# Seven block products for eight in the first FFN product of token chunks 2 and 3

## Chip, cores and metric

The kernel runs on one core of a Trainium2 chip. The metric is device time in microseconds. Where "clock" is given it is the granted TensorE clock, 1.0 being full speed.

## The reference, cut to what matters

```python
# x: 1 x 2048 x 640; wqkv: 640 x 1920; wo: 640 x 640; w1: 640 x 1728; w2: 1728 x 640, all bf16
xn = _layernorm(x)
q, k, v = split_heads(xn @ wqkv)                    # 32 heads of 20
phi = lambda t: where(t > 0, t + 1, exp(t)) + 1e-6
pq, pk = phi(q), phi(k)
kv  = einsum("bhsd,bhse->bhde", pk, v)
z   = einsum("bhsd->bhd", pk)                       # sum of the keys over all tokens
num = einsum("bhqd,bhde->bhqe", pq, kv)
den = einsum("bhqd,bhd->bhq", pq, z)[..., None] + 1e-6
s = merge_heads(num / den) @ wo
h = maximum(xn @ w1, 0)                             # the first FFN product
g = silu(h @ w2)
return x + s * g
```

The 2048 tokens are 16 tiles of 128, or four chunks (0 to 3) of 512. The kernel computes `h` transposed, in blocks of 128 of w1's columns by one chunk: five matmuls of 512 columns each, since 640 = 5 x 128.

## The kernel before

A small scheduler gives each operation the waits that its reads and writes need; each engine works through its own queue in the order of the program. These parts matter (cuts marked `# ...`).

```python
# z: the running sum of the key tiles, one GpSimd addition for each of the 16 tiles
def z_add():
    t = zpend.pop(0)
    sc.op("POOL", lambda eng: eng.tensor_tensor(out=zacc, in0=zacc, in1=pk[:, t, :], op=ALU.add), ...)

def K_fin(t):                      # phi of a key tile, two VectorE instructions with all inputs in SBUF
    sc.op("DVE", ... tensor_scalar(out=e_, in0=e_, scalar1=1.0, scalar2=1e-6, op0=ALU.min, op1=ALU.add) ...)
    sc.op("DVE", ... tensor_tensor(out=pk[:, t, :], in0=e_, in1=r_, op=ALU.add) ...)
    zpend.append(t)

def Q_block(j, f):                 # 5 matmuls, one exp on ScalarE, two VectorE instructions
    # ...                          # the second of them reads PSUM
    sc.op("DVE", ... scalar_tensor_tensor(out=pqT[:, f, schunk(j)], in0=ps[b], scalar=1.0 + 1e-6,
                                          in1=e_, op0=ALU.add, op1=ALU.max) ...)

def H_block(j, f):                 # 5 matmuls and one relu on ScalarE: a block of h
    # ...

# where things stand: chunk j's H blocks with Q blocks between them; key tiles, statistics and z by position
kat = [{5: 4, 7: 5, 9: 6, 11: 7}, {7: 8, 11: 9, 15: 10, 19: 11}, {6: 12, 9: 13, 12: 14, 15: 15}, {}]
lnat = [{}, {0: 8, 3: 9, 6: 10, 9: 11}, {0: 12, 2: 13, 4: 14, 6: 15}, {}]
zfrom = [9, 99, 10, 0]
for j in range(J):
    for n, item in enumerate(plans[j]):
        # ... Q_block or H_block, LN_stats, LN_norm, K_mm, K_exp, K_relu, K_fin
        if n >= zfrom[j] and zpend and j < J - 1:
            z_add()
        # ...
        if j == J - 1:
            while zpend:
                z_add()
            if n == 1:
                z_split()          # z as a sum of two bf16 numbers
            # ...
            if n == 9:
                z_col()            # ten one-column matmuls turn z into a column
```

The Gram product later in the kernel already uses a seven-product scheme (`seven`).

## Time and profile before

| | kernel before |
|---|---|
| time, median of runs | 210.3 us (209.55 to 210.85) |
| span of the profiled run | 208.9 us |
| TensorE busy | 205.2 us (98%), 1,377 matmuls |
| VectorE busy | 160.3 us (77%) |
| ScalarE busy | 109.7 us (53%) |
| GpSimd busy | 45.8 us (22%) |

TensorE is the bound. (PSUM, below, is the memory that matmuls write to; SBUF is the other on-chip memory.) This is GpSimd's timeline of the kernel before (start, duration, line, operation, out<-in, shapes, count):

```profile
73.28 18.19 POOL L528 TENSOR_TENSOR wv_sb<-wv_sb,reg 128x640 f32<-128x640 f32 x12
```

And this is VectorE's timeline of the same kernel, inside that time (a bracket at the end gives the idle time before the instruction and who ended it):

```profile
80.74 0.33 DVE L550 TENSOR_SCALAR regE<-regE 128x640 bf16<-128x640 bf16 x1 [1.29 <-ACT regE L534]
81.40 1.26 DVE L552 TENSOR_TENSOR reg<-regE 128x640 bf16<-128x640 bf16 x1 [0.34 <-ACT regE L534]
85.33 0.33 DVE L550 TENSOR_SCALAR regE<-regE 128x640 bf16<-128x640 bf16 x1 [2.67 <-ACT regE L534]
```

Twelve of the sixteen additions run in a block, and VectorE then has idle time in front of its instructions. Some are lengthened (1.26 us), some not (0.33 us), and nobody waits for them.

### The profile page before, as it was taken

The page shows a single profiled execution, that of the slowest core. Times are in us where ns is not written, and L with a number is a line of the kernel's source. Part 1 is how long each engine was busy: PE and PEld are TensorE (multiplying, and loading weights), DVE is VectorE, ACT ScalarE, POOL GpSimd, SP SyncE. Part 2 cuts the span into 40 slices and gives each one's busy share as a digit, 9 for nine tenths or more (in the row PEclk, how much of TensorE's full clock was granted, in tenths as well). Part 3 has the DMA queues.
Part 4 walks back from the last instruction along what each step waited for, and adds up shares of the span by engine and source line. Part 5 has one row for each costly group of instructions (what it writes and reads, how often), then busy time and mean ns, then how long its engine had stood idle before and what let it go on. Part 6 is the DMA issues. An engine that isn't in the chain of part 4 may idle for free.

```text
span 208.9 us, 3582 instructions
## 1 busy us (share of the span) xinstructions
PE 205.2 (98%) x1377; PEld 126.6 (61%) x1377; DVE 160.3 (77%) x321; ACT 109.7 (53%) x215; POOL 45.8 (22%) x71
## 2 busy tenths in 40 slices
PE   8999999999999999999999999999999999999995
PEld 7755554555454555444447777767777777777773
DVE  3988965798855995369597785897888989797465
ACT  5697767466565566655653424462435254353531
POOL 2278701111017399990000000000000000000001
PEclk9999999999999999999999999999999999999999
DMA  6987499221001334000189999346911010110103
GB/s 197 359 295 155 90 315 90 50 45 31 3 0 22 72 79 145 0 2 0 28 285 261 322 282 332 107 120 231 319 51 63 0 66 28 38 36 30 63 3 126
DMA packets 30359, 24.74 MB, mean 118 GB/s; under 512 B 12037, under 2 KB 30341, under 8 KB 30341
## 3 DMA queue, kind: packets, MB, share of 16 engines
q1 hardware_dynamic: 27013, 20.26, 34.8%
q10 hardware_dynamic: 3328, 4.24, 6.2%
q8 instruction: 11, 0.18, 0.4%
q14 instruction: 7, 0.06, 0.1%
HBM read 15.81 MB, written 5.24 MB: 101 GB/s over the span
## 4 chain that ended last, share of the span: by engine, by line
PE 97%; DMA 1%; DVE 1%; issue 0%
PE psT L798 40%; PE psT L591 27%; PE psT L517 11%; PE psT L570 10%; PE psT L1217 3%; PE psT L1301 2%; DMA reg<-in_A_x_dram 1%; PE psT L610 1%; PE psT L1008 1%; PE psT L491 1%; PE psT L982 1%; PE psT L703 1%; DVE stats L436 0%; DVE reg L1205 0%; DVE reg L1210 0%; DVE reg L484 0%
## 5 line engine op out<-in xcount | busy, mean ns | idle before, releaser
L591 PE MATMUL psT<-reg 128*128 128x512 bf16 x195 | 46.0, 379 | 0.0
L595 ACT ACTIVATE regH<-psT 128x512 bf16<-128x512 f32 x52 | 30.8, 602 | 17.2 <-PE psT L591 17.2
L798 PE MATMUL psT<-reg,regH 128*128 128x320 bf16 (+1 forms) x224 | 34.3, 299 | 0.0
L591 PEld LDWEIGHTS psT<-reg 128*128 128x128 bf16 x195 | 18.9, 98 | 21.8 <-issue 0.4
L798 PE MATMUL psT<-reg 128*128 128x320 bf16 (+1 forms) x164 | 27.2, 299 | 0.0
L798 PEld LDWEIGHTS psT<-reg,regH 128*128 128x128 bf16 (+1 forms) x224 | 21.9, 98 | 8.5
L1210 POOL TENSOR_TENSOR reg<-reg 128x224 bf16<-128x224 bf16 x1 | 0.6, 608 | 112.2 <-DVE reg L1205 112.2
L570 PE MATMUL psT<-reg 128*128 128x512 bf16 x100 | 24.8, 379 | 0.0
L1042 ACT ACTIVATE wv_sb<-psT 128x320 bf16<-128x320 f32 x28 | 11.3, 436 | 25.3 <-PE psT L798 15.5
L528 POOL TENSOR_TENSOR wv_sb<-wv_sb,reg 128x640 f32<-128x640 f32 x16 | 23.1, 1442 | 1.9 <-DVE reg L552 1.0
L743 DVE TENSOR_TENSOR psT<-psT,reg 128x320 f32<-128x320 f32 x30 | 14.3, 495 | 11.5 <-PE psT L798 11.2
L534 ACT ACTIVATE regE<-psT 128x640 bf16<-128x640 f32 x24 | 15.6, 701 | 9.1 <-PE psT L517 9.1
L798 PEld LDWEIGHTS psT<-reg 128*128 128x128 f16 (+1 forms) x164 | 16.0, 98 | 6.4
L805 ACT ACTIVATE psT<-psT 128x320 f32<-128x320 f32 x32 | 13.6, 426 | 10.8 <-PE psT L798 10.3
L517 PE MATMUL psT<-reg 128*128 128x320 bf16 x120 | 18.3, 299 | 0.0
L570 PEld LDWEIGHTS psT<-reg 128*128 128x128 bf16 x100 | 9.8, 98 | 11.6
L805 ACT ACTIVATE reg<-psT 128x320 f32<-128x320 f32 (+1 forms) x22 | 9.6, 435 | 13.1 <-PE psT L798 13.1
L576 ACT ACTIVATE regE<-psT 128x512 bf16<-128x512 f32 x20 | 12.0, 598 | 8.5 <-PE psT L570 8.5
L436 DVE BATCH_NORM_STATS2 stats<-reg 128x6 f32<-128x320 bf16 x32 | 14.1, 475 | 2.3 <-DMA reg<-in_A_x_dram 2.3
L517 PEld LDWEIGHTS psT<-reg 128*128 128x128 bf16 x120 | 11.7, 98 | 6.5
L577 DVE TENSOR_SCALAR regE<-regE 128x512 bf16<-128x512 bf16 x20 | 7.7, 386 | 9.6 <-ACT regE L576 9.5
L591 PE MATMUL psT<-regX,reg 128*128 128x512 bf16 x65 | 14.8, 379 | 0.0
(106 smaller groups left out, 300.0 us busy)
## 6 DMA issues: line engine op xcount, KB each, us to landing
scr<-rden SPq DMA_DIRECT2D x4, 640.0 KB, 9.4
reg<-in_A_x_dram SPq DMA_DIRECT2D x4, 640.0 KB, 6.3
out_dram<-reg SPq DMA_DIRECT2D x15, 160.0 KB, 1.9
reg<-in_A_x_dram SPq DMA_DIRECT2D x14, 160.0 KB, 3.4
reg<-scr SPq DMA_DIRECT2D x2, 640.0 KB, 7.5
regE<-scr SPq DMA_DIRECT2D x2, 640.0 KB, 8.0
reg<-in_B_w_dram ACTq DMA_DIRECT2D x1, 1040.0 KB, 6.6
reg<-in_A_wo_dram SPq DMA_DIRECT2D x6, 160.0 KB, 3.2
```

The source lines that it names most:

```text
L436: sc.op("DVE", lambda eng: eng.bn_stats(stats[:, t, a, :], xv[:, HN * a:HN * (a + 1)]), R=[("xin", t % XR)], W=[("stats", t, a)])
L517: fns.append(lambda eng, a=a, k=k, lhs=lhs: eng.matmul(ps[b + a][:, 0:HN], lhsT=lhs, rhs=wk[:, k, HN * a:HN * (a + 1)], start=(k == 0), st ...
L528: sc.op("POOL", lambda eng: eng.tensor_tensor(out=zacc, in0=zacc, in1=pk[:, t, :], op=ALU.add), R=[("zacc",), ("pk", t)], W=[("zacc",)])
L534: sc.op("ACT", lambda eng: eng.activation(out=o_.rearrange("p (a n) -> p a n", a=2), in_=ps2(b, HN), func=func, scale=scale), R=[("ps", b) ...
L570: sc.group("PE", [(lambda eng, k=k: eng.matmul(ps[b], lhsT=wq[:, k, P * f:P * (f + 1)], rhs=xnT[:, j, k, :], start=(k == 0), stop=(k == C ...
L576: sc.op("ACT", lambda eng: eng.activation(out=e_, in_=ps[b], func=ACTF.Exp), R=[("ps", b)], W=[("er_e", es)])
L591: a = sc.group("PE", [(lambda eng, k=k: eng.matmul(ps[b], lhsT=w1_col(k, P * f, P), rhs=src[:, k, :], start=(k == 0), stop=(k == C - 1))) ...
L595: sc.op("ACT", lambda eng: eng.activation(out=hT[:, f, schunk(j)], in_=ps[b], func=ACTF.Relu), R=[("ps", b)], W=[("hT", j, f)])
L743: sc.op("DVE", lambda eng: eng.tensor_tensor(out=out, in0=in0, in1=in1, op=op), R=R, W=W, extra=extra)
L798: sc.group("PE", [(lambda eng, k=k, lhs=lhs, rhs=rhs: eng.matmul(ps[b][:, 0:HN], lhsT=lhs, rhs=rhs, start=(start and k == 0), stop=(k == n ...
L805: sc.op("ACT", lambda eng: eng.activation(out=dst, in_=ps[b][:, 0:HN], func=ACTF.Copy), R=[("ps", b)], W=[dkey], extra=extra)
L1042: sc.op("ACT", lambda eng: eng.activation(out=g[:, HN * n:HN * (n + 1)], in_=ps[b][:, 0:HN], func=ACTF.Silu), R=[("ps", b)], W=[("g", sl, ...
```

## The change

The intent is to save TensorE work. Column blocks i and i + 6 of w1 (i = 0 to 5) with token chunks 2 and 3 form a two by two block product; over the first four of the five pieces of 128 it takes seven products of two matmuls for eight, and the fifth piece is added in the plain way: 18 matmuls for 20. Six such units replace 24 blocks. They need sums of blocks of w1 (`h_S`) and of x (`h_T`), so w1 is kept by pairs of column blocks (seven loads for three), and chunks 2 and 3 must be normalised, transposed and summed before the first unit. For that, the statistics and norms of tiles 8 and 9 move up into chunk 0's stage, and chunk 1's stage gets those of tiles 10 to 15 and the key tiles 8 to 15. Q's evacuation (the passes that bring a matmul's result out of PSUM) goes partly to ScalarE, and the z additions are issued after the stage. Buffers are rehoused, among them that of chunk 1's column scales and chunk 0's row scales.

```diff
-    FC = [0, 4 * P, 7 * P, FF]
-    w1_p = [reg5[:, C * FC[i]:C * FC[i + 1]]... for i in range(3)]
+    NW = 7
+    WL = [2 * P * d for d in range(NW)] + [FF]
+    w1_p = [reg5[:, C * WL[d]:C * WL[d + 1]]... for d in range(NW)]
 ...
-    w1_load(2, "ACT")
     K_relu(0, 2)
+    w1_load(3, NW, "SP", [("ACT", sc.count["ACT"] - 1)])
 ...
     # Q_block: the second pass of its evacuation moves from VectorE (PSUM) to ScalarE, VectorE adds in SBUF
+        def f_relu():
+            sc.op("ACT", ... activation(out=pqT[:, f, schunk(j)], in_=ps[b], func=ACTF.Relu) ...)
+        def f_sum():
+            sc.op("DVE", ... tensor_scalar(out=e_, in0=e_, ..., op0=ALU.min, op1=ALU.add) ...)
+            tt(pqT[:, f, schunk(j)], e_, pqT[:, f, schunk(j)], ALU.add, ...)
 ...
+    def h_S(d, i):       # sums of w1 blocks: A21 + A22, that - A11, A12 - that, A11 - A21
+    def h_T(i):          # sums of x:         B12 - B11, B22 - B12, that + B11, B21 - that
 ...
+    def h_unit(i):       # seven products; product 7 reuses the bank that the sum after product 6 reads
+        def s6():
+            mm(6, ba)
+            tt(ps[bc], ps[ba], s5, ALU.add, [("ps", ba), ("ps", bc), skey], [("ps", bc)])
+        # ...
+        def s7():
+            mm(7, ba)
+            cp(ps[bd], ("ps", bd), ba)
 ...
-    kat = [{5: 4, 7: 5, 9: 6, 11: 7}, {7: 8, 11: 9, 15: 10, 19: 11}, {6: 12, 9: 13, 12: 14, 15: 15}, {}]
-    lnat = [{}, {0: 8, 3: 9, 6: 10, 9: 11}, {0: 12, 2: 13, 4: 14, 6: 15}, {}]
-    zfrom = [9, 99, 10, 0]
-    for j in range(J):
+    kat = [{5: 4, 7: 5, 9: 6, 11: 7}, {2: 8, 5: 9, 8: 10, 11: 11, 14: 12, 16: 13, 18: 14, 20: 15}]
+    lnat = [{9: 8, 11: 9}, {0: 10, 2: 11, 5: 12, 8: 13, 11: 14, 13: 15}]
+    for j in range(2):
 ...
-            if n >= zfrom[j] and zpend and j < J - 1:
-                z_add()
 ...
+    Q_block(2, 0, 1)
+    Q_block(2, 1, 3)
+    while zpend:
+        z_add()
+    z_split()
 ...
+    for i, u in enumerate(units):        # s1 s5 [filler] s6 s2 [filler] s7 s3 s1-of-next s4
```

## The prediction

> **What bounds the kernel now.** I read the page first: busy shares, the slices, the chain that ended last.
>
> ```profile
> PE   8999999999999999999999999999999999999995
> DVE  3988965798855995369597785897888989797465
> POOL 2278701111017399990000000000000000000001
> PEclk9999999999999999999999999999999999999999
> ...
> PE 97%; DMA 1%; DVE 1%; issue 0%
> ```
>
> One digit is a fortieth of 208.9 us, 5.2 us. TensorE is full in every slice from the second on and its clock is never throttled; the chain is 97% TensorE. The chain in order of time has no gap above 0.02 us between 12 and 206 us, so today TensorE's stream of matmuls is the time. One piece of it gives the price of a matmul:
>
> ```profile
> 11.93 6.47 PE psT L591 x30
> ...
> 103.27 6.58 PE psT L591 x30
> ```
>
> 30 matmuls of 512 columns in 6.47 us are 0.216 us each. (The groups' 379 ns is latency; matmuls overlap.) In the same way ten of 320 columns take 1.36 us, 0.136 each. So every 512-column matmul that goes is worth 0.216 us, as long as nothing else begins to hold TensorE up. Next I asked which engine could. A table by stages gives VectorE's busy time:
>
> ```profile
> 32.50:58.60 26.10, 26.10 (x137) 13.29 (x136) 20.74 (x55) 16.01 (x27) 3.47 (x8) 1.00 0.20 40
> 58.60:87.80 29.20, 29.20 (x152) 14.70 (x150) 19.53 (x37) 18.50 (x31) 20.64 (x28) 1.00 0.23 57
> ```
>
> Columns after the length: TensorE, weight loads, VectorE, ScalarE, GpSimd (instructions in brackets). In the first stage VectorE is 79% busy and GpSimd idles; in the second VectorE has far fewer instructions (37 for 55) but nearly the same busy time, because GpSimd is working. The timelines of those two engines, 18 to 27 us, show why:
>
> ```profile
> 18.61 1.16 DVE L455 TENSOR_SCALAR reg<-reg,mv,rsy 128x640 bf16<-128x640 bf16 x1 [0.46 <-POOL rsy L444]
> 19.68 1.52 DVE L550 TENSOR_SCALAR regE<-regE 128x640 bf16<-128x640 bf16 x1
> 21.23 1.61 DVE L552 TENSOR_TENSOR reg<-regE 128x640 bf16<-128x640 bf16 x1
> 22.77 0.31 DVE L550 TENSOR_SCALAR regE<-regE 128x640 bf16<-128x640 bf16 x1
> 23.11 1.61 DVE L552 TENSOR_TENSOR reg<-regE 128x640 bf16<-128x640 bf16 x1
> ```
>
> ```profile
> 18.54 1.03 POOL L856 TENSOR_TENSOR wv_sb<-ident,rsy 128x512 f16<-128x512 bf16 x1
> 19.54 2.95 POOL L528 TENSOR_TENSOR wv_sb<-wv_sb,reg 128x640 f32<-128x640 f32 x2
> 22.98 1.40 POOL L528 TENSOR_TENSOR wv_sb<-wv_sb,reg 128x640 f32<-128x640 f32 x1 [0.49 <-DVE reg L552]
> 24.87 1.47 POOL L528 TENSOR_TENSOR wv_sb<-wv_sb,reg 128x640 f32<-128x640 f32 x1 [0.49 <-DVE reg L552]
> ```
>
> L550 takes 0.31 us when GpSimd waits and 1.52 when an L528 (the running sum of the keys, z) runs; L552 takes 0.49 undisturbed elsewhere and 1.61 here. Each L528 holds back one VectorE instruction until it ends, and the next L528 gets in before VectorE's next one. Five GpSimd passes here lengthen five VectorE instructions by 0.8, 1.2, 1.1, 1.1 and 1.1 us: **about 1.06 us a pass**. L579, which reads PSUM, keeps its 0.69 us while L528 runs (76.3 us).
>
> **What the Trainium skill says.** "SBUF — State Buffer", section "Who interferes with whom": VectorE and GpSimd share one port pair under an exclusive lock; a tensor_scalar in a two-port mode, or a tensor_tensor with both inputs in SBUF against a GpSimd operation that reads SBUF, waits for the whole other instruction; an instruction with one input and outside those modes doesn't. The trace agrees (0.31 against 1.52, 0.49 against 1.61, PSUM reader unchanged at 0.69). "TensorE: Matmul & The Clock Gate", section "Back-to-back issue gap": warm, about N / 2.4 + 2.5 ns isolated, 216 for 512 columns, and a sustained figure of 131. The trace has 216; the trace decides.
>
> **The change, part by part.**
> *Removed.* For chunks 2 and 3, 12 of the 13 full column blocks of w1: 24 blocks of 5 matmuls, 120 in all. They become 6 units. One has products of 2+3+3+3+2+2+2 and one tail of 1, 18 matmuls for 20. So 12 matmuls of 512 columns go: 12 x 0.216 = **2.6 us**. The fillers between them (Q blocks, the last block, the first three Gram steps) are old work. I find no other matmul more or less in the order of instructions. Floor: 210.5 - 2.6 = 207.9.
>
> *Added, ScalarE.* Per unit 3 copies of 128x512 and 2 relus for 4, so about 6 net; and each of 20 Q blocks gets a second pass (relu into pqT), 0.60 us each: some 16 us. ScalarE was 53% busy; a unit with its two fillers has 9 passes at 0.5 to 0.6 us (4.5 to 5.4) in 28 matmuls (6.0 us). Close, not a bound.
>
> *Added, VectorE.* Per unit a PSUM add twice (0.50 at 320 columns; an estimate of 0.7 at 512), a relu from PSUM (0.69) and one in SBUF (0.3): 2.4, times 6 = 14. Block sums of w1: 12 of 512 elements at 0.33 (back-to-back, as L743 into regH) = 4. Sums of x: 4 of 1024 at 0.68 = 2.7. Taken away: each Q block's L579 (0.61 back-to-back) becomes an SBUF add (0.33): -6. In all +15 on the 82.5 that it was busy up to 109.85 us. The units themselves have room: 2.4 + 2 x 0.65 for fillers + about 1.2 of other sums, 4.9 of 6.0.
>
> *Moved.* Chunks 2 and 3 must be normalised and transposed before the units, so all K blocks 8 to 15, all statistics and the Q blocks of 0 and 1 now stand inside chunk 1's stage, with block sums and scalings. And **all 16 z additions** are issued after that stage. GpSimd however runs them when its queue is free and their pk is there: its queue has only the small rsy instructions before them, so they start when the last statistics (tile 15, 14th item of the stage) are done.
>
> *When.* Stage 1 starts at 31.4 as before; adding 14 items at 1.08, four K blocks at 1.36, the broadcast 0.22 and the half block 1.1 gives 53.3 for the 14th item, about 55.8 for its rsy. VectorE up to there has some 19.5 us of work in 22, so it keeps up. From there to the first unit's PSUM sum, VectorE's queue holds 35 instructions that need the shared pair: 7 scalings and 3 block sums at 0.33, one norm 0.36, 4 key tiles at 0.76 a pair, 6 Q pairs at 0.65, 4 x-sums at 0.68: 13.3 us. TensorE wants that sum at about 73 to 74.7 us (stage 1 ends at 68.4, two Q blocks to 70.5, then the first unit's products up to the seventh). So without interference there are 4 to 5 us to spare.
>
> *With it.* In this stretch 16 additions and the 2 instructions that split z (0.72 and 1.40) all come due, twelve with their data there at once. At 1.06 us a pass they cost VectorE 18 x 1.06 = 19 us. So 55.8 + 13.3 + 19 = 88 where TensorE wants 74: a stall of about **14 us**, minus what overlaps (passes that wait for a key tile, or meet VectorE waiting). On the way ScalarE is held too: the exp of the tenth later Q block needs one of three er buffers, freed by the 15th of the 35 instructions, at 55.8 + 15 x 1.5 = 78.
>
> *Sum.* 210.5 - 2.6 + 14 = 222 if it is all paid; I take 11 and get 219. DMA (w1 in seven pieces, w2 pair by pair), the reciprocal in four parts and the Gram in halves I count as zero: w1's pieces are wanted later than the old ones landed, and w2 can come earlier.
>
> **The rivals.**
> 1. *Clean gain*: VectorE keeps up, TensorE stays gapless: 207.5 to 209.5. For it: the schedule looks carefully tuned (reciprocal cut up, Q evacuation taken off VectorE), which hints at someone who looked at such waits; the totals fit on paper (82.5 + 15, less some 12 of today's interference, is 85 us of undisturbed VectorE work in 107). Against: the lock, seen five times in a row in the kernel before, at just such a crowded place.
> 2. *The lock* (my choice): a gap on TensorE around 70 to 90 us, 213 to 225.
> 3. *Unit-internal waits*: product 7 needs the bank that the PSUM sum of product 6 reads, product 4 the copy of product 7, with 1.7 and 1.3 us of other matmuls between. A PSUM add of 0.7, or a copy of 0.6, fits if the queue ahead of it is empty. If it isn't, 0.3 to 1 us in each of 6 units: 2 to 5 us, 210 to 213.
> 4. *Late loads*: chunk 2's transposes are needed 5 us earlier (K block 8 at about 35 us for 40.2). L455 of tiles 0 to 3, on which the loads of tiles 8 to 11 wait, no longer meets z additions, so I expect it in time; otherwise 1 to 3 us.
>
> **Range and chances.** Faster by over 2% would need under 206.3, below the floor of 207.9: 0.01. Within 2% reaches to 214.7, a stall of up to 6.8 us: rival 1, 3, 4, or a lock half as costly as measured: 0.31. Slower: 0.68. The lowest tenth lies in the clean gain, so the range is 208.4 to 225.
>
> **What would show it.** Right: 512-column matmuls fewer by 12, still 0.216 apart; L558 (z additions) from about 56 us in one block to 80 or later; VectorE's short instructions there at 1.2 to 1.7 us; TensorE slices below 9 between 68 and 90 us, the chain passing to VectorE or GpSimd there, and gapless after. Wrong: z additions that start only after 70 us, or VectorE instructions that get through in twos and threes per pass; or a VectorE that is late already before 55 us; or gaps inside every unit (rival 3).

## The result

The changed kernel takes 228.78 us in the median (227.7 to 230.13, 4 runs), against 210.3 us. The ratio is 1.0885, with a 95% interval of 1.0809 to 1.096. It is slower, and by more than the range allowed.

The engines' busy digits in 40 slices of 5.7 us, and the shares of the chain that ended last, on the page of the kernel after:

```profile
PE   8998999999999018299999999999999999999995
...
DVE  3588657869999999958767995989898898897466
...
POOL 2176025521499972400000000000000000000001
PEclk9999999999999857889999999999999999999999
...
PE 69%; DVE 15%; issue 6%; DMA 4%; POOL 2%; ACT 2%; SPq 0%; DVEq 0%
```

There is a hole in TensorE's row from the 14th slice to the 17th (74 to 97 us), and only there. VectorE's row is full from the 10th slice to the 17th, and GpSimd's from the 12th, just ahead of the hole, to the 14th. TensorE's clock falls inside the hole. TensorE's share of the chain went from 97% to 69%; VectorE now has 15%. TensorE is busy for 208.3 us (91% of 228.8), VectorE for 185.3 (81%), ScalarE for 120.5 (53%), GpSimd for 47.1.

TensorE's timeline of the kernel after, through the hole:

```profile
74.03 0.59 PE L1017 MATMUL psT<-reg 128*128 128x512 bf16 x2
85.19 1.04 PE L1017 MATMUL psT<-regE,pqT 128*128 128x512 f16 x2 [10.57 <-DVE regE L807]
...
89.33 0.61 PE L1017 MATMUL psT<-regX,pqT 128*128 128x512 f16 x2 [0.96 <-ACT psT L1023]
...
95.95 1.03 PE L1017 MATMUL psT<-regX,reg 128*128 128x512 f16 x2 [4.29 <-DVE psT L807]
```

L1017 are the products of the first unit. Product 5 waits 10.57 us for the first sum of x; product 6, 0.96 us for a copy on ScalarE; product 7, 4.29 us for the PSUM sum. Each wait ends at VectorE or at something late because of it. After 96 us no unit waits. GpSimd's timeline of the kernel after:

```profile
62.31 21.18 POOL L558 TENSOR_TENSOR wv_sb<-wv_sb,reg 128x640 f32<-128x640 f32 x14
84.68 1.71 POOL L558 TENSOR_TENSOR wv_sb<-wv_sb,reg 128x640 f32<-128x640 f32 x1 [1.19 <-DVE reg L582]
```

And VectorE's timeline over the same stretch:

```profile
61.83 0.42 DVE L807 TENSOR_TENSOR regH<-regH,wv_sb 128x512 f16<-128x512 bf16 x1
62.37 1.51 DVE L485 TENSOR_SCALAR reg<-reg,mv,rsy 128x640 bf16<-128x640 bf16 x1
63.81 1.55 DVE L580 TENSOR_SCALAR regE<-regE 128x640 bf16<-128x640 bf16 x1
65.40 1.60 DVE L582 TENSOR_TENSOR reg<-regE 128x640 bf16<-128x640 bf16 x1
66.93 1.48 DVE L626 TENSOR_SCALAR regE<-regE 128x512 bf16<-128x512 bf16 x1
...
80.63 3.14 DVE L807 TENSOR_TENSOR regH<-regH,wv_sb 128x512 f16<-128x512 bf16 x2
83.70 0.31 DVE L580 TENSOR_SCALAR regE<-regE 128x640 bf16<-128x640 bf16 x1
...
95.19 0.70 DVE L807 TENSOR_TENSOR psT<-psT,reg 128x512 f32<-128x512 f32 x1
```

The block sum L807 takes 0.42 us just before GpSimd's first addition and 1.6 us after it. In GpSimd's 21.18 us of 14 additions VectorE gets through exactly 14 instructions, one for each; when the block ends L580 is back at 0.31 us. From 62.37 us to the PSUM sum at 95.19 us VectorE runs 32 instructions and waits for nobody.

The rest of the arithmetic, from this profile: 12 matmuls fewer (1,365), as intended. To tell a late start from a stall, each run's start is taken from the key product of tile 4. TensorE's timeline of the kernel before:

```profile
18.24 1.52 PE L517 MATMUL psT<-reg 128*128 128x320 bf16 x10
```

And TensorE's timeline of experiment z_none below, with the same product and the seventh product of the first unit, undisturbed:

```profile
20.02 1.53 PE L547 MATMUL psT<-reg 128*128 128x320 bf16 x10 [0.47 <-DMA reg<-reg]
...
76.48 0.59 PE L1017 MATMUL psT<-regX,reg 128*128 128x512 f16 x2
```

z_none began 20.02 - 18.24 = 1.78 us late, so its seventh product stands at 74.70 us by the kernel before's start. The kernel after began 3.43 us late (tile 4 at 21.67 us) and has its seventh product at 95.95 us. The stall is then 95.95 - 74.70 - 3.43 = 17.8 us. After it, 13 matmuls take 4.27 us from start to start (95.95 to 100.22) instead of 2.80 (z_none), most of them at half clock: 1.5 us. Sum: 3.4 + 17.8 + 1.5 - 2.6 = 20.1 us; the spans differ by 228.8 - 208.9 = 19.9.

### The profile page after: what moved, and what is told of

Same layout as the page of the kernel before. It is cut to its first block, busy times and chain, and to the rows that moved or that the text cites. A ratio compares the mean times of both kernels' runs of the same rounds, so it can differ in the third digit from the quotient of the medians. Undisturbed runs are those within 1.5% of the kernel's fastest.

```text
span 228.8 us, 3679 instructions
## 1 busy us (share of the span) xinstructions
PE 208.3 (91%) x1365; PEld 127.4 (56%) x1365; DVE 185.3 (81%) x364; ACT 120.5 (53%) x242; POOL 47.1 (21%) x71
## 4 chain that ended last, share of the span: by engine, by line
PE 69%; DVE 15%; issue 6%; DMA 4%; POOL 2%; ACT 2%; SPq 0%; DVEq 0%
PE psT L862 36%; PE psT L1017 10%; PE psT L654 7%; PE psT L547 5%; PE psT L605 4%; DVE regH L807 3%; PE psT L1475 2%; DMA reg<-reg 2%; DVE regE L626 2%; DMA reg<-in_A_wqkv_dram 2%; PE psT L1527 2%; POOL rsy L465 2%; DVE stats L457 2%; DVE regE L580 2%; DVE pqT L807 1%
## 5 line engine op out<-in xcount | busy, mean ns | idle before, releaser
L862 PE MATMUL psT<-reg 128*128 128x320 bf16 (+1 forms) x164 | 27.7, 299 | 0.0
L605 PE MATMUL psT<-reg 128*128 128x512 bf16 x100 | 25.8, 392 | 0.0
L558 POOL TENSOR_TENSOR wv_sb<-wv_sb,reg 128x640 f32<-128x640 f32 x16 | 23.3, 1455 | 6.3 <-DVE reg L582 5.3
L1300 ACT ACTIVATE wv_sb<-psT 128x320 bf16<-128x320 f32 x28 | 11.3, 436 | 25.2 <-PE psT L862 15.2
L807 DVE TENSOR_TENSOR psT<-psT,reg 128x320 f32<-128x320 f32 (+1 forms) x33 | 16.3, 512 | 9.8 <-PE psT L862 8.9
L869 ACT ACTIVATE reg<-psT 128x320 f32<-128x320 f32 (+1 forms) x24 | 10.5, 436 | 15.6 <-PE psT L862 13.6
L654 PE MATMUL psT<-reg 128*128 128x512 bf16 x75 | 18.5, 379 | 0.0
L658 ACT ACTIVATE regH<-psT 128x512 bf16<-128x512 f32 x28 | 16.6, 611 | 3.3 <-PE psT L654 3.3
L605 PEld LDWEIGHTS psT<-reg 128*128 128x128 bf16 x100 | 10.0, 101 | 11.8 <-issue 1.8
L807 DVE TENSOR_TENSOR reg<-reg 128x1024 f16<-128x1024 bf16 (+6 forms) x17 | 14.7, 877 | 1.5 <-DMA reg<-in_B_w_dram 0.8
L457 DVE BATCH_NORM_STATS2 stats<-reg 128x6 f32<-128x320 bf16 x32 | 14.1, 474 | 2.2 <-DMA reg<-in_A_x_dram 2.2
L547 PEld LDWEIGHTS psT<-reg 128*128 128x128 bf16 x120 | 11.7, 98 | 7.5 <-DMA reg<-reg 1.2
L807 DVE TENSOR_TENSOR pqT<-regE,pqT 128x512 bf16<-128x512 bf16 x20 | 13.1, 655 | 2.2 <-ACT pqT L618 1.6
```

The lines of the kernel that those rows point to most:

```text
L457: sc.op("DVE", lambda eng: eng.bn_stats(stats[:, t, a, :], xv[:, HN * a:HN * (a + 1)]), R=[("xin", t % XR)], W=[("stats", t, a)])
L547: fns.append(lambda eng, a=a, k=k, lhs=lhs: eng.matmul(ps[b + a][:, 0:HN], lhsT=lhs, rhs=wk[:, k, HN * a:HN * (a + 1)], start=(k == 0), st ...
L605: sc.group("PE", [(lambda eng, k=k: eng.matmul(ps[b], lhsT=wq[:, k, P * f:P * (f + 1)], rhs=xnT[:, j, k, :], start=(k == 0), stop=(k == C ...
L654: sc.group("PE", [(lambda eng, k=k: eng.matmul(ps[b], lhsT=w1_col(k, P * f, P), rhs=src[:, k, :], start=(k == 0), stop=(k == C - 1))) for ...
L658: return lambda: sc.op("ACT", lambda eng: eng.activation(out=hT[:, f, schunk(j)], in_=ps[b], func=ACTF.Relu), R=[("ps", b)], W=[("hT", j, f)])
L807: sc.op("DVE", lambda eng: eng.tensor_tensor(out=out, in0=in0, in1=in1, op=op), R=R, W=W, extra=extra)
```

## The experiments

Two theories, and a third that came with the result. **Lock**: the z additions on GpSimd and VectorE's instructions that need the port pair (the one that the prediction describes) hold each other up, one for one, at the place where VectorE has no slack. **Schedule**: the new stage is too full for VectorE (or the units' own waits, or the later loads) and the additions only keep it company. **Clock**: part of the loss is the half clock after the idle time.

### z_none: the additions taken away (wrong result)

```diff
-    while zpend:
-        z_add()
+    zpend.clear()
     z_split()
```

`zacc` is set to 1000 instead of 0, so that nothing divides by zero.

> The 16 z additions on GpSimd are left out (z is a constant, so the result is wrong on purpose); everything else stands. Theory (shared port lock): each addition holds back one VectorE instruction by about 1.1 us, so without them the short VectorE instructions fall back to 0.3 to 0.5 us, the gaps on TensorE between the first unit's first and seventh product (15.8 us in the changed kernel) shrink to under 1.5 us, and the half clock after them (3.1 us) goes too: 228 - 18 = 208 to 212 us. Rival (VectorE has too much work of its own in chunk 1's stage): a gap of 5 us or more stays at the same place, 215 us or more.

Measured: 208.85 us (208.11 to 209.53), ratio 0.9915 (0.9852 to 0.9978), clock 1.0, no gap on TensorE at the units. VectorE's timeline of z_none, the same place of the program:

```profile
58.52 0.88 DVE L457 BATCH_NORM_STATS2 stats<-reg 128x6 f32<-128x320 bf16 x2
...
60.73 0.45 DVE L485 TENSOR_SCALAR reg<-reg,mv,rsy 128x640 bf16<-128x640 bf16 x1
61.09 0.32 DVE L580 TENSOR_SCALAR regE<-regE 128x640 bf16<-128x640 bf16 x1
61.44 0.49 DVE L582 TENSOR_TENSOR reg<-regE 128x640 bf16<-128x640 bf16 x1
...
72.25 1.48 DVE L626 TENSOR_SCALAR regE<-regE 128x512 bf16<-128x512 bf16 x1
...
75.13 0.70 DVE L807 TENSOR_TENSOR psT<-psT,reg 128x512 f32<-128x512 f32 x1 [0.28 <-PE psT L1017]
```

The same 32 instructions take 14.1 us (60.73 to 74.85) instead of 32.8, and VectorE now waits for TensorE at the PSUM sum, though only for 0.28 us. The one instruction of 1.48 us meets the split of z, which was left in. So the additions are the cause: with them gone the schedule holds, and Schedule falls as the main cause. The price of an addition is (32.8 - 14.1) / 16 = 1.17 us. The new schedule is also worth having in itself: 1.6 us under the 210.42 us of the kernel before in the same rounds.

### z_half: eight additions instead of sixteen (wrong result)

```diff
+    zpend[:] = [t for t in zpend if t % 2 == 0]
     while zpend:
         z_add()
```

> Only the 8 additions of the even tiles are done (wrong result on purpose), at the same place in GpSimd's queue; the split stays. Theory (lock, so much per pass): 8 passes fewer give VectorE back 8 x 1.1 = 9 us before the first unit's PSUM sum, and the half clock after the wait goes with the shorter wait: 217 to 220 us. Rival (the wait comes from a few particular passes, or the additions cost nothing until some threshold): 210 or 227.

Measured: 219.2 us (218.78 to 221.57), ratio 1.0438 (1.0379 to 1.0498). The three doses, 0, 8 and 16 additions, give 208.85, 219.2 and 228.78 us: nearly a straight line, 10.35 us for the first eight and 9.6 for the rest. In its VectorE timeline the 32 instructions run from 61.11 to 84.54 us: (23.4 - 14.1) / 8 = 1.16 us an addition again. The loss comes addition by addition, with no threshold; there was no slack of the predicted 4 to 5 us to swallow the first few (with the split alone, in z_none, 0.28 us was left before the PSUM sum). One part of the expectation failed: the half clock did not go with the shorter wait. In this profile, of the slowest of the four runs, the 13 matmuls from the seventh product take 5.52 us for 2.80, so the three times contain some clock too; the 1.16 us does not.

### z_gate: all additions, but after the first unit's sum

The additions are issued in the first unit, and each waits for the VectorE instruction issued just before it, so the first cannot start before that PSUM sum.

```diff
-    while zpend:
-        z_add()
-    z_split()
 ...
         u["s6"]()
+        if i == 0:
+            while zpend:
+                z_add()
+            z_split()
```

with `extra=[("DVE", sc.count["DVE"] - 1)]` added to `z_add`'s waits.

> The 16 additions stay on GpSimd, but the first one waits for the first unit's PSUM sum on VectorE, so that they run beside the units and no longer beside chunk 1's stage. Theory (lock; VectorE has 4.9 of 6.0 us to do in a unit and each pass adds 1.1): the gap in the first unit goes, but units 1 to 4 stretch, and z comes late for the den: 216 to 223 us. Rival (only the place was unlucky, the units have room): 209 to 212.

Measured: 220.87 us (220.53 to 221.06), ratio 1.0484 (1.0422 to 1.0546). The first unit starts without a wait; two of the next ones stall for long. (Units 1 to 4 were expected to stretch and z to come late; its ten matmuls begin at 107.13 us without a wait.) TensorE's timeline of z_gate:

```profile
83.72 2.31 PE L605 MATMUL psT<-reg 128*128 128x512 bf16 x5 [2.86 <-DVE regH L1032]
...
96.10 2.31 PE L605 MATMUL psT<-reg 128*128 128x512 bf16 x5 [4.60 <-DVE regH L1032]
```

The block of additions starts at 75.17 us instead of 62.31. That moves the stall and lessens it: 12.0 us over z_none instead of 19.9, some half clock after the waits included. The result is right, and the same sixteen additions are done. So what they cost depends on what slack VectorE has where they run, and inside the units it has too little.

### z_pe: z on TensorE

The tensor engine can sum the key tiles itself: 80 one-column matmuls, accumulated in PSUM, for the ten of `z_col`. GpSimd's additions and the split go. The result is right.

```diff
-        sc.group("PE", [(... matmul(ps[b][:, c:c + 1], lhsT=zhl[:, a, P * c:P * (c + 1)], rhs=ones[:, :],
-                                    start=(a == 0), stop=(a == 1))) for c in range(C) for a in range(2)], ...)
+        sc.group("PE", [(... matmul(ps[b][:, c:c + 1], lhsT=pk[:, t, P * c:P * (c + 1)], rhs=ones[:, :],
+                                    start=(t == 0), stop=(t == T - 1))) for c in range(C) for t in range(T)], ...)
-    while zpend:
-        z_add()
-    z_split()
+    zpend.clear()
```

> z is summed on TensorE (80 matmuls of one column with the keys as weights, in the place of the 10 that read z) and not on GpSimd; the result is right. Ten such matmuls took 0.23 us, so 70 more cost about 1.6 us. Theory (lock): as without the additions, plus 1.6: 209.5 to 213.5 us, so about level with the kernel before, where the 2.6 us that the seven products save are nearly used up. Rival (VectorE's own work): 216 or more.

Measured: 211.15 us (210.62 to 212.4), ratio 1.0033 (0.9966 to 1.01), level with the kernel before. The piece of the chain of z_pe that pays for it (start, duration, matmuls):

```profile
95.92 1.98 PE psT L753 x80
```

80 matmuls in 1.98 us are 25 ns each. This repairs the changed kernel to within noise of the one before, and gives back most of the 2.6 us that the seven products save.

### q_old: Q's evacuation as before, z on TensorE

One line of z_pe: `plain = False`, which puts the second pass of each Q block back on VectorE, reading PSUM.

> z on TensorE as in z_pe (211.2), and the Q blocks evacuated as before the change: one ScalarE pass and a VectorE instruction that reads PSUM (0.69 us for 0.43). Without the lock VectorE has some 4 us to spare in chunk 1's stage and about 1 us in a unit; 20 x 0.28 more, of it 12 before the units: the slack just holds it, 211 to 213. Rival (the move of the Q evacuation to ScalarE is what makes the units run without gaps): 214 or more, with gaps in every unit.

Measured: 211.03 us (209.9 to 211.34), ratio 1.0017 (0.9961 to 1.0073). Without the lock the move of Q's evacuation to ScalarE buys nothing that these runs can show. VectorE is busy for 18.33 of the 20 us from 60 to 80 us instead of 16.13 in z_pe, and still TensorE does not wait. Not tested is the old evacuation with the additions left in: its second instruction reads PSUM and kept its 0.69 us beside an addition in the kernel before (76.33 us), so with the lock the move may have made the stall longer.

### b_zpe: the kernel before with z on TensorE

The edit of z_pe, made to the kernel before; the result is right.

> The kernel before with z summed on TensorE in place of GpSimd's additions (right result). Theory: there the lock lengthened VectorE instructions too, but off the path, so that taking the additions away gains nothing, and the 70 more small matmuls cost 1.6 to 1.8 us: 211.5 to 212.7, ratio 1.006 to 1.010. Rival (the lock cost time before as well): below 210.5.

Measured: 212.86 us (211.76 to 213.81, 6 runs), ratio 1.0117 (1.0074 to 1.0159): 2.4 us slower, not faster, where the extra matmuls account for an estimated 1.75 us (70 at the 25 ns of z_pe); the median is just above the expected range. So the additions cost the kernel before nothing that these runs can show, although they lengthened many of VectorE's instructions there: the L552 of 1.26 us at 81.40 us takes 0.49 us in b_zpe. That is the half of the lesson that the totals hide: the same sixteen additions cost nothing measurable in one schedule and 20 us in the other.

### warm: useless matmuls in the gaps

44 matmuls of 512 columns before the first unit's fifth product and 12 before its seventh keep TensorE busy where it waits. They write to a bank that is not read. The result is right.

```diff
+        if i == 0:
+            warm(44)
 ...
+        if i == 0:
+            warm(12)
```

> 56 matmuls without use (512 columns) are put where TensorE waits in the first unit, 44 before the fifth product and 12 before the seventh, so that it never idles for long. Theory (a part of the loss is the clock, granted at half after the long wait: 3.1 us in the trace): 2 to 3.5 us less than the changed kernel, 224.5 to 226.5, with clock 1.00 there and the same VectorE times. Rival (the clock costs nothing, as TensorE only waits there for VectorE): no change, 228.

Measured: 227.15 us (226.69 to 228.06), ratio 1.0777 (1.0701 to 1.0853). The gain of 1.6 us is less than the 2 to 3.5 us expected, and it compares medians of different rounds (warm's slowest run, 228.06 us, is above the fastest of the changed kernel), so it rests on the trace. TensorE's timeline of warm:

```profile
91.43 2.75 PE L1187 MATMUL psT<-reg,const-bfloat16-1.0 128*128 128x512 bf16 x12
94.20 0.60 PE L1017 MATMUL psT<-regX,reg 128*128 128x512 f16 x2
```

The seventh product starts at 94.20 us, 19.89 us being this run's start of tile 4's product: relative to that start no earlier than in the kernel after (95.95 - 21.67 = 74.28; 94.20 - 19.89 = 74.31). So what TensorE did at half clock before that point was hidden behind VectorE. Only the matmuls after it, now at full clock (0.60 us for two, where it was 1.03; 13 in 2.82 us for 4.27), were worth something. (The gaps were not filled throughout: the clock still fell to 0.76 in the mean from 85 to 90 us.) The Clock theory is right in kind, with some 1.5 us.

### after2: the changed kernel once more

> The changed kernel once more, unaltered, for a second profile of it. The first profile fell on the slowest of its runs (230.1 us), with tile 4's key product at 21.67 us, 3.3 us later than before. If that start is chance, this profile has it at 19.0 to 20.5 us, and the first unit's PSUM sum moves forward by as much, so that the stall of some 17.7 us before the seventh product keeps its length within 1 us; time 227 to 230. If the late start were part of the change, it would stand at 21 us or later again.

Measured: 228.92 us (227.32 to 230.11), ratio 1.0899 (1.0845 to 1.0953); this profile fell on a run of 228.56 us, near the median. TensorE's timeline of after2:

```profile
19.61 1.53 PE L547 MATMUL psT<-reg 128*128 128x320 bf16 x10 [0.57 <-DMA reg<-reg]
...
94.26 0.64 PE L1017 MATMUL psT<-regX,reg 128*128 128x512 f16 x2 [2.51 <-DVE psT L807]
```

The start is 1.37 us late, not 3.43, so three fifths of the first profile's late start are chance. Most of that difference of 2.1 us, 1.8 us, lies between 6 and 11.3 us, where the first profile's matmuls ran longer: eight of 320 columns in 2.34 us, in 1.37 here. The stall is 94.26 - 74.70 - 1.37 = 18.2 us, as long as before. With 1.7 us of half clock (13 matmuls in 4.50 us against 2.80 in z_none, starts read from the timelines) the sum is 1.4 + 18.2 + 1.7 - 2.6 = 18.7; the spans differ by 227.3 - 208.9 = 18.4.

### w1_rows: longer rows in the first load of w1

z_pe with the first four column blocks of w1 in one load, its rows 1,024 bytes long as in the kernel before instead of 512. (The first pair of w2's blocks, which takes that buffer, is then loaded two units later.)

```diff
-    w1_load(0, 2, "SP")
+    dma("SP", lambda eng: eng.dma_start(w1_01, B_w1[:, 0:4 * P]....), W=[("w1", 0), ("w1", 1)])
```

> z on TensorE as in z_pe, and the first four blocks of w1 loaded in one transfer with rows of 1024 bytes, as before the change, instead of two with rows of 512. Theory (the small rows of w1 hold up the keys' weights, on which TensorE waits 0.2 to 1.2 us at 5 us, and the first transposes, 0.5 us at 19 us): K of tile 4 starts at 18.4 to 18.9 us instead of 19.3 to 21.7, and the time falls by about 1 us to 209.5 to 210.6. Rival (the late start has another cause, or is chance): no change, 211.

Measured: 210.96 us (209.73 to 211.81, 6 runs), ratio 1.0025 (0.9982 to 1.0068); tile 4's product at 19.62 us. A miss: the row length is not why the changed kernels begin late. Two waits remain: 0.92 us for the first part of wk at 6 us, and 0.45 us for the transposed x of tile 4. The first is not the change's at all, since b_zpe, whose loads are those of the kernel before, shows it too (1.08 us).

### w1_act: w1's last loads back on ScalarE's queue

```diff
+    w1_load(3, NW, "ACT")
     K_relu(0, 2)
-    w1_load(3, NW, "SP", [("ACT", sc.count["ACT"] - 1)])
```

z_pe otherwise.

> z_pe (z summed on TensorE by 80 one-column matmuls) with one thing put back to the kernel before: w1's last four pieces are loaded on the ScalarE queue right after the first exp, as before, and not on the SP queue ahead of the transposes of x. It tests why the key product of tile 4 started at 19.0 to 21.7 us in every changed kernel and at 18.4 in the kernel before. If the place of these loads is the cause, the ten matmuls of tile 4 begin without a wait for the transposed x, at or before 18.9 us, and the time is some 0.5 us under that of z_pe: 210.2 to 210.9. If the late start is scatter of the first loads or has another cause, the wait of 0.35 to 0.6 us for the transposed x stays and the time is as z_pe's, 210.7 to 211.6.

Measured: 211.53 us (210.07 to 212.38, 6 runs), ratio 1.0061 (1.0026 to 1.0096); tile 4's product at 18.86 us. The two lines that tell why, from the timeline of w1_act, ScalarE's queue and TensorE:

```profile
9.37 2.12 ACTq L377 DMA_DIRECT2D reg<-in_B_w_dram  x4
...
12.38 6.65 PE L653 MATMUL psT<-regX,reg 128*128 128x512 bf16 x30 [0.61 <-ACT regE L563]
```

The wait for the transposed x is gone, as expected if the loads ahead of the transposes caused it. But issuing four loads takes ScalarE 2.12 us in the middle of the key tiles' evacuation, and TensorE waits 0.61 us for that instead. The time does not fall. The kernel before has one load there, of 0.39 us; cutting w1 into more pieces seems to make one of the two waits due. This rests on one profile of each (w1_act's is of the fastest of its six runs), and half a microsecond is near the scatter.

## Why the prediction was wrong

The mechanism was the one predicted; four terms of the sum were too small or missing. The largest is the step "VectorE up to there has some 19.5 us of work in 22, so it keeps up", on which the 4 to 5 us to spare rested: VectorE was some 3.5 us behind, and the stall was 18.2 us where 14 stood. The second is the last step, "222 if it is all paid; I take 11 and get 219": it was all paid, 3 us more. The clock (1.7 us) and the late start (1.4) were counted as nothing. For the median run, with after2's profile:

| Step, as the prediction put it | predicted | measured |
|---|---|---|
| "12 matmuls of 512 columns go" | -2.6 us | 12 fewer; z_none is 1.6 us under the kernel before, though its profile starts 1.8 us late |
| TensorE wants the sum "at about 73 to 74.7 us" | 74 | product 7 at 74.70, late start taken off |
| "so it keeps up": the last statistics and their rsy (a GpSimd step that the norm waits for) done | 55.8 us | 60.65 in after2, of which 1.37 is the late start; 3.5 behind |
| the 35 instructions without interference | 13.3 us | 32 instructions, 14.1 with the two split passes (z_none), some 12.5 without |
| "18 x 1.06 = 19 us" | 19 | 16 x 1.17 + 1.6 for the split = 20.3 |
| "minus what overlaps" | -3 | 0 |
| clock | not named | +1.7 |
| loads "I count as zero" | 0 | late start +1.4 (3.4 in the slowest run) |

- **Overlap.** The prediction allowed for passes that meet VectorE waiting. There was none: from 62.37 us on VectorE's queue always held a ready instruction, so each of the 18 GpSimd passes, two of them the split's, lengthened one VectorE instruction. This is 3 us of the miss, and z_half shows that it holds dose by dose.
- **"So it keeps up".** It was argued from a sum over the whole stretch, 19.5 us of work in 22. In the undisturbed z_none VectorE is busy for 6.74 of the 10 us from 40 to 50 us and for 9.36 of the 10 from 50 to 60 us: the work is bunched at the end, where the last statistics are. TensorE is where the prediction had it: in z_none it is through the 14th item of the stage at 55.07 us, 53.3 without the late start. But VectorE, which waits for nobody from 50.9 us on, begins the last statistics only at 58.52 us. So the queue was late already, without any addition (their rsy ends at 60.69 us, 1.8 of it the late start). A VectorE "that is late already before 55 us" stood among the prediction's own signs of being wrong, and came true. Of the 4 to 5 us to spare about 2.6 were left (an estimate: 74 - 58.9 - 12.5). The size of the bunch is measured; which instruction of it would have to move was not tried.
- **The two sizes of the lock.** 1.17 us a pass for 1.06, on 12.5 us of bare work for 13.3. By luck these nearly cancel: 32.8 us measured, 13.3 + 19.1 = 32.4 predicted.
- **Clock.** This stall was not over when the data came. The prediction's trace showed a clock that was "never throttled", because TensorE was never idle in it; it did not ask what ten idle microseconds would do.
- **Loads.** The changed kernels begin 0.6 to 1.8 us later, and in one profile 3.4. Part is chance, a wait for wk that the kernel before can have too (b_zpe, with the old loads, begins 0.8 us late). Part is the place of w1's loads, for w1_act removed the wait for the transposed x. Its exact share stays open.

Adding up: 219 + 3 (overlap) + 4.2 (a stall of 18.2 where 14 stood, most of it the lateness) + 1.7 (clock) + 1.4 (start) = 229.3, against 228.78.

Of the rivals, the clean gain is what z_none shows when the lock is gone. Unit-internal waits did not come: after the seventh product no unit waits. Late loads were right in kind at the start of the kernel.

No right version beat the kernel before beyond the noise. z_pe and q_old are level with it: the seven products save 2.6 us, z on TensorE costs an estimated 1.75 us more than the ten matmuls it replaces (70 x 25 ns), and the start costs about one.

## What to carry to other kernels

When two engines share a lock, the price is not set by how often they meet but by whether the longer one has work waiting where the other has no slack: the same sixteen additions cost nothing measurable in one schedule and 20 us in the next. So when a change packs a stage, look for the operations that it moved along without mention, and check slack where the last of the packed work is due, not on the average of the stage. And do not discount a queue's work for overlap unless the profile shows idle time for it to overlap with.

## What the Trainium skill lacked or had wrong

- "SBUF — State Buffer", section "Who interferes with whom": the lock is as the page says, and these runs agree (instructions of 0.28 to 0.49 us became 1.48 to 1.62; in z_gate one that reads PSUM kept 0.68 between lengthened ones). It lacks what happens when both queues are full: they alternate one for one, 14 VectorE instructions in 14 additions, and each addition costs VectorE 1.17 us, while the mean addition itself takes 1,455 ns here and 1,442 ns in the kernel before. It lacks the other case too: the same additions cost nothing measurable where VectorE was idle in between (b_zpe).
- "TensorE: Matmul & The Clock Gate", section "What's actually happening": the fall to half clock after at least one idle window of some 3.4 us agrees with the trace (in the kernel after TensorE is idle from 74.6 us, and the granted clock is 0.85 in the mean from 75 to 80 us and 0.50 from 80 to 85, so the fall came an estimated 3.9 us after the last matmul). It lacks which part of the half clock a stall pays: here only the matmuls after the wait that ends last, 1.5 to 1.7 us, while the stretch before was hidden (warm).
- The same page, section "Back-to-back issue gap": the sustained 131 ns for 512 columns was not seen; the stream of 30 took 216 ns each. The 25 ns floor for one column was: 80 in 1.98 us.
- No page gives a time measured on trn2 for issuing a load from ScalarE's queue: four loads held ScalarE for 2.12 us (w1_act), one took 0.39 us (the kernel before).
